# Attention and two feed-forward layers on one core: how the decay rows and the first q and k are brought in

## The chip, the cores and the metric

The kernel runs on one core of one Trainium2 chip. The metric is the device time of one execution in microseconds (us); the time before is the median of three runs. A core has five engines that work side by side, each through its own list of instructions in order: TensorE (PE in the profile, with its weight loads as PEld), VectorE (DVE), ScalarE (ACT), GpSimd (POOL) and SyncE (SP), which here issues transfers only.

## What is computed

Cut to what matters, with B, H, S, D = 4, 8, 576, 64, a model width of 512 and an inner width of 2048:

```python
scores = (q @ k.transpose(0, 1, 3, 2)) / sqrt(D)
log_f = log(clip(f, 1e-4, 1.0))              # f: [B, H, S]
cum = cumsum(log_f, axis=-1)
decay = cum[:, :, :, None] - cum[:, :, None, :]
scores = where(causal, -1e9, scores + decay)
attn = softmax(scores)                       # sum + 1e-9
x = (attn @ v)  as [B*S, H*D] = [2304, 512]
h = x @ w1_in;  g = h * tanh(softplus(h));  y = g @ w1_out
h = y @ w2_in;  g = h * cos(h);             out = g @ w2_out
```

q, k, v and f come as float32; the four weight matrices come as 64-bit floats, which the kernel takes apart into two float32 numbers each.

## The kernel before

**Jobs.** Attention goes by jobs: one pair of heads of one batch (`jobs`, L385 to L388). In batch 0 each pair is cut into two jobs, of query blocks 0 and 1 and of blocks 2, 3 and 4, so that the first four jobs need columns 0 to 255 only; in the other batches a pair is one job of 576 queries. That makes 20 jobs. `span` (L396) gives a job's batch, pair, first query and last key.

**The stacked operand.** The decay is added within the score product. For each job there is a tile `stk` of [128, 2 heads, 2, 576], two in a ring (`ring`, L635), in which index 0 of the third axis is for the queries and 1 for the keys. Rows 0 to 63 hold q (times 0.125) or k with the head's width along the rows; row 64 and row 96 hold the running sum `cum` or constants, so that the product adds cum of the query and takes off cum of the key. All other rows from 64 on are set by memsets once at the start (L639 to L642): 0, 0, -1 and 1. The product (`scores`, L501) runs over all 128 rows.

**Decay rows before.** `decay_tables` (L712) loads f as [32, 576], clips it (L716), takes the logarithm (L717) and the running sum over 576 columns (L719). `prep_job` begins with two transfers of one row each (L449, L450) for its own job: from the table in SBUF for job 0, for all others from `cumd`, a copy of the table in DRAM that job 0's preparation writes (L452).

**A job's preparation.** `load_job` (L401) brings q and k of a job as they lie; `prep_job` (L441) transposes them on TensorE (L468) into a PSUM bank and copies the result into `stk`, the queries of the first head on VectorE (L486), the other three parts on ScalarE (L484). At its end it starts the loads of v for the next job and of q and k for the job behind that. It is a generator, run a step at a time in the last steps of the job before. `load_v` (L420) brings v, which is needed by the product with the probabilities (`av`, L602).

**Softmax.** Per block: the score products, then on VectorE the mask, the negated values and the row minimum in one instruction (L529), on ScalarE the exponential with the row sum (L534), the reciprocal on VectorE, the scaling on GpSimd (L548), transposes on TensorE (L575, L591), copies of these into the tile `p` of probabilities (L567 on ScalarE, L569 on VectorE), and the product with v (L613).

**Weights.** `split_weights` (L88) brings weights in pieces into three buffers `raw` (L104); each piece takes three instructions on VectorE (L123, L124, L133), one on GpSimd (L128) or ScalarE, one on ScalarE (L137) and one on GpSimd (L138). The first pieces are converted between the softmax steps. Their loads are issued after the copy of the table to DRAM (`marks["cum"]`, L107).

**The order.** The main loop (L771 on) mixes attention steps, weight pieces and steps of the first feed-forward layer, by a credit per attention step. Within this a scheduler orders the instructions of every engine when the program is built; an engine then runs its list strictly in that order, and so does SyncE with the transfers that it issues. A transfer also waits until the one eight places ahead of it has landed.

Of the kernel before, what the change touches and what calls it, by code (L numbers as in the profile page):

```python
# [9 lines left out]
F32 = mybir.dt.float32  # L10
F32R = mybir.dt.float32r
I32 = mybir.dt.int32
AF = mybir.ActivationFunctionType
ALU = mybir.AluOpType
# [22 lines left out]
def tile_attention_two_ffn(  # L37
# [12 lines left out]
    nc = tc.nc  # L50
    B, H, S, D = q.shape
# [25 lines left out]
    xd = dram.tile([128, 2, NK, NT], F32, name="xd")  # L77
    yd = dram.tile([128, 2, NK, NT], F32, name="yd")
    pd = dram.tile([128, NK, NT], F32, name="pd")
    cumd = dram.tile([B * H, S], F32, name="cumd")  # L80


    W = {}
# [300 lines left out]
    def attention_units(p, bank):  # L384
# [16 lines left out]
        def load_job(jb):  # L401
            if jb >= len(jobs):
                return
            b, hp, qlo, khi, last = span(jb)
            hs = slice(2 * hp, 2 * hp + 2)
            ts = []
            for nm, src, lo in (("q", q, qlo), ("k", k, 0)):
                P, C = SPLIT[khi - lo]
                t = p.tile([128, 6, 2, D], F32, tag=f"nat{nm}", name=f"nat{nm}", bufs=2)
                if jb == 0:  # L410
                    nc.sync.dma_start(out=t[0:P, 0:C], in_=src[b, hs, lo:khi].rearrange("h (p c) d -> p c h d", c=C))
                else:
                    for j in range(2):
                        nc.sync.dma_start(
                            out=t[0:P, 0:C, j], in_=src[b, 2 * hp + j, lo:khi].rearrange("(c p) d -> p c d", c=C)
                        )
                ts.append(t)
            nat[jb] = ts

        def load_v(jb):  # L420
# [17 lines left out]
                        )  # L438
            vt[jb] = t

        def prep_job(jb):  # L441
            if jb >= len(jobs):
                return
            b, hp, qlo, khi, last = span(jb)
            qn, kn = nat.pop(jb)
            st = ring[jb % len(ring)]
            h0 = b * H + 2 * hp
            src = cums[0][h0 : h0 + 2] if jb == 0 else cumd[h0 : h0 + 2]
            nc.sync.dma_start(out=st[96:97, :, 0], in_=src)  # L449
            nc.sync.dma_start(out=st[64:65, :, 1], in_=src)  # L450
            if jb == 0:
                marks["cum"] = nc.sync.dma_start(out=cumd, in_=cums[0])  # L452
            yield
            cols = []
            for which, src, lo in ((0, qn, qlo), (1, kn, 0)):
# [9 lines left out]
            for g in groups:  # L465
# [3 lines left out]
                for which, lo in ((0, qlo), (1, 0)):  # L469
# [5 lines left out]
                    for j in range(2):  # L475
                        i_ = t[64 * j : 64 * j + 64, at : at + n * P]
                        if jb == 0:
                            o = st[0:64, j, which, lo:khi].rearrange("r (p c) -> r c p", c=C)[:, c0 : c0 + n]
                            i_ = i_.rearrange("r (c p) -> r c p", p=P)
                        else:  # L480
                            o = st[0:64, j, which, lo + c0 * P : lo + (c0 + n) * P]
                        sc = 0.125 if which == 0 else 1.0
                        if which or j:
                            nc.scalar.activation(out=o, in_=i_, func=AF.Copy, scale=sc)  # L484
                        else:
                            nc.vector.tensor_scalar(out=o, in0=i_, scalar1=sc, scalar2=None, op0=ALU.mult)  # L486
                yield
            if jb:
                load_v(jb + 1)
            load_job(jb + 2)  # L490

        def scores(jb, i):
# [6 lines left out]

            def product(o, j, c0, c1):  # L500
                marks["score"] = nc.tensor.matmul(  # L501
                    o, lhsT=st[:, j, 0, qs], rhs=st[:, j, 1, c0:c1], start=True, stop=True
                )

            heads = []
# [127 lines left out]
            nc.sync.dma_start(out=xd[:, :, hp, b * S + qlo : b * S + khi], in_=f(xs.pop(jb)[:, :, qlo:khi]))  # L633

        ring = []  # L635
        for i in range(2):
            ring.append(p.tile([128, 2, 2, S], F32, name=f"stk{i}", bufs=1))
            en = nc.vector if i == 0 else nc.gpsimd
            nc.gpsimd.memset(ring[-1][96:128, :, 0], 0.0)  # L639
            nc.gpsimd.memset(ring[-1][64:96, :, 1], 0.0)  # L640
            en.memset(ring[-1][64:96, :, 0], -1.0)
            en.memset(ring[-1][96:128, :, 1], 1.0)  # L642
            if i == 0:
                make_masks()
        for jb in range(2):
            load_job(jb)
        load_v(0)
        load_v(1)
        for _ in prep_job(0):
            pass  # L650
        prep = None
# [39 lines left out]
            nxt = [e for e in ends if e > m]  # L691
            yield ("step", m, nxt[0] - m if nxt else 1)

    nc.scalar.preload_act_table_set("natural_log_exp_and_others")
    make_identity(nc, ident)
    nc.gpsimd.memset(two, 2.0)
    nc.gpsimd.memset(quarter, 0.25)

    def make_masks():
        nc.gpsimd.memset(maskt, 0.0)  # L700
        nc.gpsimd.affine_select(
# [9 lines left out]

    def decay_tables(p):  # L712
        NH = B * H
        ft, cum, one = (p.tile([128, S], F32, tag="s", name="s", bufs=7)[0:NH] for _ in range(3))
        nc.sync.dma_start(out=ft, in_=fg.rearrange("b h s -> (b h) s"))
        nc.vector.tensor_scalar(out=ft, in0=ft, scalar1=1e-4, scalar2=1.0, op0=ALU.max, op1=ALU.min)  # L716
        nc.scalar.activation(out=ft, in_=ft, func=AF.Ln)  # L717
        nc.gpsimd.memset(one, 1.0)
        nc.vector.tensor_tensor_scan(out=cum, data0=one, data1=ft, initial=0.0, op0=ALU.mult, op1=ALU.add)  # L719
        cums.append(cum)  # L720

    NA = 8
    first = [(TA * i, TA, 2) for i in range(NA)]
# [38 lines left out]
    def bank():  # L762
        return psa.tile([128, 512], F32, tag="s1", name="s1")

    decay_tables(ap)
    att = attention_units(ap, bank)
    w1a = weights = split_weights(1, lo, w0p)
    done_tokens, attention_over, pos = 0, False, 0
    psf, credit = None, 0.0
# [75 lines left out]
```

## Time and profile before

| | |
|---|---|
| median of three runs | 1099.02 us (1098.57 to 1100.02) |
| the profiled execution's own time | 1097.69 us |
| its span, first to last instruction | 1095.9 us |
| mean granted TensorE clock | 0.998 |
| VectorE busy, share of the span | 637.9 us, 58% |
| ScalarE busy | 563.5 us, 51% |
| GpSimd busy | 232.8 us, 21% |
| packets of the transfers, share of 16 engines | 32.9% |

Times in the rows further down are in us from the start of the span. An instruction's line (L501) is its line in the kernel before. A float32 product shows as two records. "x4" are instructions of a kind that follow each other, merged into one row, with the time from the first one's start to the last one's end or their sum. The releaser named behind an idle time is inferred from the semaphores.

### The profile page before, as it was taken

Reading aid. Unit: us, or ns where it says so; the run is one execution under the profiler, and the core shown is the slowest. Engines: PE = TensorE matmul, PEld = TensorE weight load, DVE = VectorE, ACT = ScalarE, POOL = GpSimd, SP = SyncE. Lnnn points to the kernel's source line nnn. Section 1 sums busy time; section 2 is a strip of 40 time slices with the busy share of each in tenths; the row PEclk is TensorE's granted clock in tenths of the full one; section 3 lists DMA queues with packets and bytes.
Section 4 is the critical chain, followed back from the end, with each engine's and each line's share of the span. In section 5 each row is a group of like instructions: output and inputs, shape, how many; then the busy total and the mean of one; then the engine's idle time right before and its main releaser. Section 6 shows DMA issues by size and latency. Waiting matters only on the chain.

```text
span 1095.9 us, 17795 instructions
## 1 busy us (share of the span) xinstructions
PE 1062.1 (97%) x6496; PEld 936.1 (85%) x6496; DVE 637.9 (58%) x1461; ACT 563.5 (51%) x1196; POOL 232.8 (21%) x267
## 2 busy tenths in 40 slices
PE   5899999999999999999999999999999999999998
PEld 4575787688878889999999999889999999999987
DVE  5769675677547575543555525995444454454543
ACT  4676676766666564443444424665334343343432
POOL 6647532333322323221111101330000000000000
PEclk9999999999999999999999999999999999999999
DMA  5845522532251135454555535432010020100000
GB/s 138 218 116 151 173 56 75 156 85 55 75 151 35 56 131 182 166 193 130 159 188 185 180 121 188 155 105 87 1 58 30 1 87 1 58 29 1 31 1 29
DMA packets 119415, 110.54 MB, mean 101 GB/s; under 512 B 65168, under 2 KB 101520, under 8 KB 119328
## 3 DMA queue, kind: packets, MB, share of 16 engines
q1 hardware_dynamic: 119328, 109.41, 32.9%
q8 instruction: 51, 0.84, 0.3%
q14 instruction: 36, 0.29, 0.1%
HBM read 80.99 MB, written 28.39 MB: 100 GB/s over the span
## 4 chain that ended last, share of the span: by engine, by line
PE 85%; DVE 8%; issue 2%; ACT 2%; DMA 1%; SPq 1%; POOL 0%; ACTq 0%; POOLq 0%; DVEq 0%
PE h L205 20%; PE acc L227 17%; PE acc L236 17%; PE hx L205 14%; PE s L501 7%; PE s L613 5%; PE s L591 4%; PE s L468 1%; DVE raw L123 1%; DVE s L529 1%; DVE raw L124 1%; DVE raw L133 1%; ACT stk L484 1%; DMA xd<-xs 0%; DVE r L325 0%
## 5 line engine op out<-in xcount | busy, mean ns | idle before, releaser
L205 PE MATMUL h<-x,wih 128*128 128x384 f32 (+1 forms) x1056 | 242.1, 317 | 0.0
L343 DVE TENSOR_TENSOR gl<-e,gh 128x384 fp32r<-128x384 f32 (+1 forms) x157 | 108.6, 692 | 141.2 <-ACT gh L335 140.6
L205 PEld LDWEIGHTS h<-x,wih 128*128 128x128 f32 x1056 | 180.8, 189 | 8.7 <-issue 2.6
L205 PE MATMUL h<-x,wil 128*128 128x384 f32 (+1 forms) x528 | 167.5, 317 | 0.2 <-POOL wil L138 0.2
L205 PE MATMUL hx<-x,wih 128*128 128x384 f32 (+1 forms) x672 | 166.1, 328 | 0.0
L335 ACT ACTIVATE gh<-e 128x384 fp32r<-128x384 f32 (+1 forms) x180 | 97.8, 544 | 101.8 <-DVE e L331 53.8
L227 PE MATMUL acc<-gl,woh 128*128 128x256 f32 (+1 forms) x480 | 148.7, 310 | 0.0
L227 PE MATMUL acc<-gh,woh 128*128 128x256 f32 (+1 forms) x480 | 148.5, 312 | 0.0
L227 PE MATMUL acc<-gh,wol 128*128 128x256 f32 (+1 forms) x480 | 147.5, 308 | 0.0
L548 POOL TENSOR_SCALAR s<-s,sm 128x448 f32<-128x448 f32 (+5 forms) x144 | 92.1, 655 | 155.8 <-DVE sm L546 49.6
L501 PE MATMUL s<-stk 128*128 128x192 f32 (+7 forms) x384 | 111.9, 420 | 13.3 <-DMA stk<-s 4.5
L205 PEld LDWEIGHTS hx<-x,wih 128*128 128x128 f32 x672 | 120.1, 188 | 4.2
L236 PE MATMUL acc<-woh,gl 128*128 128x512 f32 x288 | 113.3, 397 | 3.1 <-DVE gl L343 3.1
L236 PE MATMUL acc<-wol,gh 128*128 128x512 f32 x288 | 113.7, 395 | 0.0
L236 PE MATMUL acc<-woh,gh 128*128 128x512 f32 x288 | 112.3, 390 | 0.8 <-DVE part L272 0.8
L205 PE MATMUL hx<-x,wil 128*128 128x384 f32 (+1 forms) x336 | 110.4, 328 | 0.0
L534 ACT ACTIVATE s<-s,mx 128x448 f32<-128x448 f32 (+5 forms) x144 | 83.5, 581 | 45.9 <-DVE mx L529 44.8
L205 PEld LDWEIGHTS h<-x,wil 128*128 128x128 f32 x528 | 99.8, 189 | 1.6 <-issue 0.6
L316 ACT ACTIVATE n<-n 128x384 f32<-128x384 f32 x96 | 50.4, 525 | 87.1 <-DVE n L305 87.1
L227 PEld LDWEIGHTS acc<-gl,woh 128*128 128x128 f32 x480 | 90.9, 189 | 2.6 <-issue 0.7
L227 PEld LDWEIGHTS acc<-gh,woh 128*128 128x128 f32 x480 | 90.7, 190 | 2.4 <-issue 1.1
L227 PEld LDWEIGHTS acc<-gh,wol 128*128 128x128 f32 x480 | 91.0, 190 | 1.8 <-issue 0.9
(88 smaller groups left out, 1669.1 us busy)
## 6 DMA issues: line engine op xcount, KB each, us to landing
raw<-in_moe_w_in_dram SPq DMA_DIRECT2D x32, 512.0 KB
raw<-in_moe_w_out_dram SPq DMA_DIRECT2D x32, 512.0 KB
x<-xd SPq DMA_DIRECT2D x6, 1536.0 KB
x<-yd SPq DMA_DIRECT2D x6, 1536.0 KB
x<-xd SPq DMA_DIRECT2D x8, 1024.0 KB
xd<-xs SPq DMA_DIRECT2D x12, 576.0 KB
natk<-in_k_dram SPq DMA_DIRECT2D x32, 144.0 KB
pd<-part SPq DMA_DIRECT2D x18, 256.0 KB
```

The source lines that it names most:

```text
L123: nc.vector.tensor_scalar(out=low, in0=low, scalar1=29, scalar2=None, op0=ALU.logical_shift_right)
L205: nc.tensor.matmul(o, lhsT=a[wsl], rhs=b[:, kk, :], start=(kk == 0 and i == 0), stop=(kk == NK - 1 and i == 2),)
L227: nc.tensor.matmul(o, lhsT=a[dsl], rhs=b[:, gs], start=(start and i == 0 and d % nsub == 0), stop=(end and i == 2), skip_group_check=True,)
L236: nc.tensor.matmul(acc[ti][m], lhsT=a[:, ms], rhs=b[:, j, :], start=(start and i == 0), stop=(end and i == 2),)
L316: nc.scalar.activation(out=t, in_=t, func=AF.Sin, scale=TWO_PI)
L335: nc.scalar.activation(out=gh, in_=e, func=AF.Copy)
L343: marks["v1"] = nc.vector.tensor_tensor(out=gl, in0=st[n][0], in1=f(gst[n][0]), op=ALU.subtract)
L501: marks["score"] = nc.tensor.matmul(o, lhsT=st[:, j, 0, qs], rhs=st[:, j, 1, c0:c1], start=True, stop=True)
L534: nc.scalar.activation(out=s[:, 0:w], in_=s[:, 0:w], func=AF.Exp, scale=-1.0, bias=mx, accum_out=sm[:, j : j + 1])
L548: nc.gpsimd.tensor_scalar(out=s[:, 0:w], in0=s[:, 0:w], scalar1=sm[:, j : j + 1], scalar2=1.0, op0=ALU.mult, op1=ALU.mult)
L591: nc.tensor.transpose(t[:, 128 * x : 128 * x + 128], ss[j][:, QS[c] : QS[c] + 128], ident)
L613: nc.tensor.matmul(t[64 * j : 64 * j + 64, c0:width], lhsT=vt[jb][0:kr, c, j], rhs=pt[0:kr, j, c, c0:width], start=(c == 0), stop=(c == nb ...
```

## The change

First, q and k of job 0 are issued by ScalarE, ahead of everything else that it does. Second, the rows move: `stk` now uses row 64 and row 65 only, the product runs over 66 rows, and there is one memset of -1 and one of 1 per ring tile. Jobs 0 and 1 get their rows from the table in SBUF, one row per transfer and only the columns that the job needs; from job 2 on there is one transfer per job from a DRAM table that holds both rows with their constants (`cumd`, now [2, 32, 2, 576], written by four transfers). A job's rows are asked for at the end of the preparation of the job before it, not at the start of its own. Third, clip, logarithm and running sum go by two parts, columns 0 to 255 and 256 to 575. Also, the copy of k for the first head of job 0 goes to VectorE, and masks, loads and memsets of the start stand in another order in the source.

```diff
-    cumd = dram.tile([B * H, S], F32, name="cumd")
+    cumd = dram.tile([2, B * H, 2, S], F32, name="cumd")
...
                 if jb == 0:
-                    nc.sync.dma_start(out=t[0:P, 0:C], in_=src[b, hs, lo:khi].rearrange("h (p c) d -> p c h d", c=C))
+                    nc.scalar.dma_start(out=t[0:P, 0:C], in_=src[b, hs, lo:khi].rearrange("h (p c) d -> p c h d", c=C))
...
+        def load_rows(jb):
+            if jb >= len(jobs):
+                return
+            b, hp, qlo, khi, last = span(jb)
+            st = ring[jb % len(ring)]
+            h0 = b * H + 2 * hp
+            if jb < 2:
+                for which in range(2):
+                    nc.sync.dma_start(out=st[64 + which : 65 + which, :, which, 0:khi], in_=cums[0][h0 : h0 + 2, 0:khi])
+            else:
+                nc.sync.dma_start(
+                    out=st[64:66].rearrange("x j w s -> x (j w s)"),
+                    in_=cumd[:, h0 : h0 + 2].rearrange("x j w s -> x (j w s)"),
+                )
+
+        def store_tables():
+            cum, one, less = cums
+            for x, which, src in ((0, 0, cum), (0, 1, one), (1, 0, less), (1, 1, cum)):
+                marks["cum"] = nc.sync.dma_start(out=cumd[x, :, which], in_=src)
...
-            h0 = b * H + 2 * hp
-            src = cums[0][h0 : h0 + 2] if jb == 0 else cumd[h0 : h0 + 2]
-            nc.sync.dma_start(out=st[96:97, :, 0], in_=src)
-            nc.sync.dma_start(out=st[64:65, :, 1], in_=src)
             if jb == 0:
-                marks["cum"] = nc.sync.dma_start(out=cumd, in_=cums[0])
+                load_rows(0)
             yield
...
-                        if which or j:
+                        if j if jb == 0 else which or j:
                             nc.scalar.activation(out=o, in_=i_, func=AF.Copy, scale=sc)
...
+            load_rows(jb + 1)
+            if jb == 0:
+                store_tables()
+                load_v(1)
             if jb:
                 load_v(jb + 1)
...
-                    o, lhsT=st[:, j, 0, qs], rhs=st[:, j, 1, c0:c1], start=True, stop=True
+                    o, lhsT=st[0:66, j, 0, qs], rhs=st[0:66, j, 1, c0:c1], start=True, stop=True
...
+        load_job(0)
+        yield ("begun", 0)
         for i in range(2):
...
-            nc.gpsimd.memset(ring[-1][96:128, :, 0], 0.0)
-            nc.gpsimd.memset(ring[-1][64:96, :, 1], 0.0)
             en.memset(ring[-1][64:96, :, 0], -1.0)
-            en.memset(ring[-1][96:128, :, 1], 1.0)
-            if i == 0:
-                make_masks()
-        for jb in range(2):
-            load_job(jb)
+            en.memset(ring[-1][64:96, :, 1], 1.0)
+        make_masks()
+        load_job(1)
         load_v(0)
-        load_v(1)
...
-        nc.vector.tensor_scalar(out=ft, in0=ft, scalar1=1e-4, scalar2=1.0, op0=ALU.max, op1=ALU.min)
-        nc.scalar.activation(out=ft, in_=ft, func=AF.Ln)
         nc.gpsimd.memset(one, 1.0)
-        nc.vector.tensor_tensor_scan(out=cum, data0=one, data1=ft, initial=0.0, op0=ALU.mult, op1=ALU.add)
-        cums.append(cum)
+        nc.gpsimd.memset(less, -1.0)
+        for c0, c1 in ((0, 256), (256, S)):
+            c = slice(c0, c1)
+            nc.vector.tensor_scalar(out=ft[:, c], in0=ft[:, c], scalar1=1e-4, scalar2=1.0, op0=ALU.max, op1=ALU.min)
+            nc.scalar.activation(out=ft[:, c], in_=ft[:, c], func=AF.Ln)
+            nc.vector.tensor_tensor_scan(
+                out=cum[:, c], data0=one[:, c], data1=ft[:, c], initial=cum[:, c0 - 1 : c0] if c0 else 0.0,
+                op0=ALU.mult, op1=ALU.add,
+            )
+        cums.extend((cum, one, less))
```

The built order at three places. First, SyncE's list from its start to the first weights, before; `s` is the tile of gates or of their sums, `stk_99` and `stk_115` are the two ring tiles, for jobs 0, 2, ... and 1, 3, ...:

```order
L715 DMA s<-in_f_dram 32x576
L411 DMA natq<-in_q_dram 64x8x64
L411 DMA natk<-in_k_dram 64x8x64
L414 DMA natq<-in_q_dram 64x4x64 x2
L414 DMA natk<-in_k_dram 64x4x64 x2
L436 DMA natv<-in_v_dram 128x2x64 x4
L449 DMA stk_99<-s 1x2x576
L450 DMA stk_99<-s 1x2x576
L452 DMA cumd<-s 32x576
L414 DMA natq<-in_q_dram 64x4x64 x2
L414 DMA natk<-in_k_dram 64x4x64 x2
L449 DMA stk_115<-cumd 1x2x576
```

The same place now (`stk_108` is the tile of jobs 0, 2, ..., `stk_111` that of jobs 1, 3, ...; L449 and L451 are the two transfers of `load_rows`):

```order
L727 DMA s<-in_f_dram 32x576
L414 DMA natq<-in_q_dram 64x4x64 x2
L414 DMA natk<-in_k_dram 64x4x64 x2
L436 DMA natv<-in_v_dram 128x2x64 x2
L449 DMA stk_108<-s 1x2x256 x2
L449 DMA stk_111<-s 1x2x256 x2
L459 DMA cumd<-s 32x576 x4
L436 DMA natv<-in_v_dram 128x2x64 x2
L414 DMA natq<-in_q_dram 64x4x64 x2
L414 DMA natk<-in_k_dram 64x4x64 x2
L104 DMA raw<-in_moe_w_in_dram 128x2x512 x2
L104 DMA raw<-in_moe_w_out_dram 128x1024
```

The two loads of job 0 have left SyncE; two of the four loads of v stand behind the rows, and the rows of both first jobs ahead of the table stores. Right behind these rows the list goes on so, with the row transfer of job 2 directly behind the weights, and that of job 3 behind the loads of job 3:

```order
L451 DMA stk_108<-cumd 2x2304
L414 DMA natq<-in_q_dram 64x4x64 x2
L414 DMA natk<-in_k_dram 64x4x64 x2
L451 DMA stk_111<-cumd 2x2304
L414 DMA natq<-in_q_dram 80x4x64 x2
```

In the list before, the two row transfers of job 2 stood behind the loads of job 3 (L414), which stood behind the weights.

Second, VectorE at the first piece of weights (`raw`), before; the copies L486 go into `stk`, here that of job 2, and L529 is the mask and minimum, here of job 1's two blocks:

```order
L529 ISA s,mx<-s_229,maskt 128x128
L529 ISA mx 128x1
L123 TENSOR_SCALAR raw<-raw 128x512
L486 TENSOR_SCALAR stk_99<-s_246 64x256
L124 SCALAR_TENSOR_TENSOR raw<-raw 128x512
L545 TENSOR_SCALAR sm<-sm 128x2
L123 TENSOR_SCALAR raw<-raw 128x512
```

The same place now (L549 is the mask and minimum, L589 the copy of transposed probabilities, L502 the copy into `stk`):

```order
L549 ISA s,mx<-s_271,maskt 128x256
L549 ISA mx 128x1
L123 TENSOR_SCALAR raw<-raw 128x512
L589 COPY p<-s_293 128x2x128
L502 TENSOR_SCALAR stk_108<-s_249 64x256
L124 SCALAR_TENSOR_TENSOR raw<-raw 128x512
L565 TENSOR_SCALAR sm<-sm 128x2
```

Job 1's second block (`s_271`, 256 columns) is now reduced ahead of the first weight operation, and a copy of probabilities stands between that and job 2's copy.

Third, TensorE at the same time, before; L468 are the transposes of q and k, L501 the score products, L591 the transposes of probabilities:

```order
L501 MATMUL s_229<-stk_115 128x128 x2
L468 MATMUL s_246<-ident,natq 128x64 x4
L468 MATMUL s_246<-ident,natk 128x64 x4
L501 MATMUL s_268<-stk_115 128x256 x2
L591 MATMUL s_289<-ident,s 128x128 x2
L501 MATMUL s_298<-stk_99 128x128 x2
```

And now (L484, L521 and L611 in their place):

```order
L521 MATMUL s_234<-stk_111 128x128 x2
L484 MATMUL s_249<-ident,natq 128x64 x4
L521 MATMUL s_271<-stk_111 128x256 x2
L611 MATMUL s_293<-ident,s 128x128 x2
L484 MATMUL s_249<-ident,natk 128x64 x4
L521 MATMUL s_302<-stk_108 128x128 x2
```

The transposes of k for job 2 have moved behind job 1's second block; job 2's first products come last in both. Further on the lists differ in small exchanges of neighbours only, and from some 280 us of the trace before on, TensorE's list is the same.

## Rows read from the trace of the kernel before

**Rows 1.** The page, totals: busy time (share of the span) and instructions by engine.

```profile
PE 1062.1 (97%) x6496; PEld 936.1 (85%) x6496; DVE 637.9 (58%) x1461; ACT 563.5 (51%) x1196; POOL 232.8 (21%) x267
```

**Rows 2.** Table by stages: length, PE, PEld, DVE, ACT, POOL busy, PEclk, DMA share, GB/s.

```profile
30.00:60.00 30.00, 25.94 (x172) 18.62 (x171) 21.99 (x74) 21.39 (x57) 18.95 (x23) 0.94 0.78 202
...
130.00:200.00 70.00, 69.38 (x493) 53.33 (x493) 43.99 (x151) 47.07 (x121) 22.16 (x33) 1.00 0.35 90
```

**Rows 3.** Timeline, 0 to 13 us: start, length, instruction, [idle before, releaser].

```profile
0.72 1.28 ACT L694 ACT_TABLE_LOAD   x1 [0.72 <-PEq L830]
0.73 0.40 SPq L715 DMA_DIRECT2D s<-in_f_dram  x1
1.19 0.73 SPq L411 DMA_DIRECT2D natq<-in_q_dram  x1
1.96 0.64 SPq L411 DMA_DIRECT2D natk<-in_k_dram  x1
...
3.00 1.05 POOL L640 MEMSET stk<- 32x1152 f32 x1
3.38 0.98 DVE L716 TENSOR_SCALAR s<-s 32x576 f32<-32x576 f32 x1
...
4.39 0.68 ACT L717 ACTIVATE s<-s 32x576 f32<-32x576 f32 x1 [2.38 <-DVE s L716]
...
5.16 0.69 PE L468 MATMUL s<-ident,natk 64*128 64x64 f32 x4 [0.30 <-DMA natk<-in_k_dram]
5.18 1.35 DVE L719 TENSOR_TENSOR_SCAN s<-s 32x576 f32<-32x576 f32 x1 [0.82 <-POOL mask L705]
...
5.31 2.14 SPq L436 DMA_DIRECT2D natv<-in_v_dram  x4
...
7.06 1.89 ACT L484 ACTIVATE stk<-s 64x256 f32<-64x256 f32 x3 [1.99 <-DVE stk L486]
...
8.44 0.62 SPq L450 DMA_DIRECT2D stk<-s  x1
...
9.81 0.53 POOL L707 TENSOR_SCALAR_AFFINE_SELECT mask<-mask 64x64 f32<-64x64 f32 x2
...
10.30 1.19 PE L501 MATMUL s<-stk 128*128 128x128 f32 x4 [4.46 <-DMA stk<-s]
```

**Rows 4.** Timeline, 13 to 25 us: the first weights, and job 2's copies and first products.

```profile
13.77 0.91 SPq L104 DMA_DIRECT2D raw<-in_moe_w_in_dram  x2
...
17.74 0.43 DVE L123 TENSOR_SCALAR raw<-raw 128x512 int32<-128x512 int32 x1 [0.83 <-DMA raw<-in_moe_w_in_dram]
...
18.08 0.41 DVE L486 TENSOR_SCALAR stk<-s 64x256 f32<-64x256 f32 x1
...
18.58 1.19 ACT L484 ACTIVATE stk<-s 64x256 f32<-64x256 f32 x3 [0.96 <-DVE stk L486]
...
23.06 1.20 PE L501 MATMUL s<-stk 128*128 128x128 f32 x4 [3.28 <-DMA stk<-cumd]
```

**Rows 5.** Chain of waits, 0 to 90 us: start, length, what the end waited for.

```profile
18.73 4.20 DMA stk<-cumd
...
70.50 4.59 DMA xd<-xs
```

**Rows 6.** TensorE: two timeline rows, then the stage table (length, busy, PEclk, DMA share, GB/s).

```profile
12.46 2.07 PE L501 MATMUL s<-stk 128*128 128x256 f32 x4
...
31.76 1.05 PE L501 MATMUL s<-stk 128*128 128x256 f32 x4
...
30.80:47.90 17.10, 13.42 (x86) 1.00 0.86 218
...
48.00:51.00 3.00, 2.72 (x6) 0.50 0.43 98
```

**Rows 7.** TensorE's weight loads by form, 130 to 383 us: busy us, mean ns | idle before.

```profile
L591 PEld LDWEIGHTS s<-ident,s 128*128 128x128 f32 x298 | 32.6, 140 | 10.0 <-issue 6.8 <-POOL s L548 1.2
L468 PEld LDWEIGHTS s<-ident,natk 96*128 96x128 f32 x60 | 6.5, 140 | 0.1
```

More of the change, by code (lines that the diff above doesn't have):

```diff
@@ L692, in attention_units @@
             yield ("step", m, nxt[0] - m if nxt else 1)
[L694 to L697, printed above, removed]
     def make_masks():
@@ L713, in decay_tables @@
         NH = B * H
-        ft, cum, one = (p.tile([128, S], F32, tag="s", name="s", bufs=7)[0:NH] for _ in range(3))
+        ft, cum, one, less = (p.tile([128, S], F32, tag="s", name="s", bufs=7)[0:NH] for _ in range(4))
         nc.sync.dma_start(out=ft, in_=fg.rearrange("b h s -> (b h) s"))
-        nc.vector.tensor_scalar(out=ft, in0=ft, scalar1=1e-4, scalar2=1.0, op0=ALU.max, op1=ALU.min)
-        nc.scalar.activation(out=ft, in_=ft, func=AF.Ln)
         nc.gpsimd.memset(one, 1.0)
-        nc.vector.tensor_tensor_scan(out=cum, data0=one, data1=ft, initial=0.0, op0=ALU.mult, op1=ALU.add)
-        cums.append(cum)
+        nc.gpsimd.memset(less, -1.0)
[8 more added lines that the diff above has]
+        cums.extend((cum, one, less))
     NA = 8
@@ L763, in bank @@
         return psa.tile([128, 512], F32, tag="s1", name="s1")
+    att = attention_units(ap, bank)
+    next(att)
+    nc.scalar.preload_act_table_set("natural_log_exp_and_others")
+    make_identity(nc, ident)
+    nc.gpsimd.memset(two, 2.0)
+    nc.gpsimd.memset(quarter, 0.25)
     decay_tables(ap)
-    att = attention_units(ap, bank)
     w1a = weights = split_weights(1, lo, w0p)
```

## The prediction

> **What bounds the kernel now.** The engine totals come first: TensorE is busy for 1062.1 us of a span of 1095.9 us [rows 1], so a change that touches no matrix product of the two feed-forward layers can move little beyond the 33.8 us in which it is idle. The table by stages says where those lie: from 130 to 200 us 0.62 of 70 us are idle, from 30 to 60 us alone 4.06 of 30 [rows 2]. So the end is set by how soon TensorE is fed without gaps, and all that follows is about the first 130 us.
>
> The timeline of the start comes next; a row's bracket says how long the engine was idle before it and what ended that. TensorE stands idle for 4.46 us until the first job's decay rows have landed. The path to them: VectorE's clip of the gates at 3.38 us, logarithm 0.68, running sum 1.35 us, over at 6.53. But SyncE issues four loads of v first (5.31 to 7.45), the second of the two row transfers goes out at 8.44, and the first product starts at 10.30, 1.86 us after it [rows 3]. The timeline from 13 us on has the other large gap, 3.28 us: the third job's copies are over at 19.77 us (18.58 + 1.19), yet its product waits until 23.06 for rows of the table [rows 4]; in the chain of waits that transfer is one piece of 4.20 us from 18.73 on [rows 5].
>
> **The change, part by part.**
>
> *First q and k on ScalarE.* q is issued at 1.19 us on SyncE, behind the gates, and k 0.77 later [rows 3]. On ScalarE I expect 0.73, as the gates have it, and 1.50, so both land 0.46 us sooner: k, whose transposes start at 5.16, at 4.7. No row shows an issue on ScalarE; SyncE's go from 0.40 to 0.73 us [rows 3], and I take the 0.73, of the same transfer. Two of them stand before the activation table load of 1.28 us, which then ends near 3.5; the logarithm has its input at 3.85, and that covers it. A rule speaks against this part: the Trainium skill, DMA: Bandwidth & Descriptors, section Issuing engines are not separate DMA queues, has it that issuing from a second engine saves only the time of issuing. By it q and k gain the same 0.46 us; if the row were to show a shorter flight as well, the sum would not change, because the rows land last either way.
>
> *Decay sums in two parts.* Taken by columns from [rows 3]: clip 0.45 and 0.55, logarithm 0.35 and 0.43, sum 0.60 and 0.75 us. The first clip runs from 3.38 to 3.85, the first logarithm to 4.25, the second clip to 4.45, the first sum from 4.50 to 5.15, where the whole sum ended at 6.53. The starts of the three extra instructions lie within the rounding; the second sum falls between two copies.
>
> *First rows from SBUF, 256 columns.* SyncE issues the gates, four loads for job 1 (0.65 each) and two loads of v, and is free at 4.95 instead of 7.45 us. Rows go out at 5.2 and 5.95 and land at 5.95 + 1.86 = 7.8 us. The first job's copies alternate in the built program, each waiting for the one before: VectorE 5.4 to 5.95, ScalarE (0.63, a third of 1.89) to 6.6, the second sum on VectorE to 6.75, its second copy to 7.3, ScalarE's second to 7.95. So the first product starts near 8.1 us, 2.2 us sooner. GpSimd loses four memsets of 1.05 us ahead of the masks and gains one of half that size; the masks, over at 10.34 us before (9.81 + 0.53), are ready near 6.7, which the first product covers.
>
> *One row transfer per job, a job earlier.* Two issues become one in 18 jobs, and three table stores are added (0.40, as the gates' issue). On SyncE the first weights now stand behind four row transfers, four stores, two loads of v and four of q and k: 7.95 + 1.7 + 1.0 + 2.6 gives 13.3 us, against 13.77 [rows 4]. The transfer for job 2 follows the three weight loads, at 14.7 us; what it waits for, the second block's products of job 0, ended at 14.53 before [rows 6] and should end at 12.3. No row shows a transfer of two pieces of 9 KB. The nearest are 1.73 us on quiet queues (the 1.86 less 0.13 until the product starts [rows 3]) and 4.20 and 4.59 us under load [rows 5]: it lands between 16.4 and 19.3 us. I take 19, since it flies among weights. Behind it on SyncE stand the loads of job 3, not needed before 20 us.
>
> What is late next for job 2 is its copies. VectorE takes its instructions in order: the first weight operation, which waited 0.83 us for its load until 17.74 [rows 4], then a copy out of the bank of probabilities, and only then the copy for job 2. With the load 0.5 us sooner and job 1's reductions now ahead of it, the weight operation runs from 17.4 to 17.8, the other copy to 18.3, the copy for job 2 (0.41) to 18.8, ScalarE's three (1.19) to 20.0, and the product starts at 20.2 instead of 23.06: 2.9 us sooner. The gain of the start is inside this, not beside it.
>
> *66 rows in the score products, not 128.* TensorE's weight loads of 96 rows take 140 ns, those of 128 rows 140 [rows 7]: nothing.
>
> *Sum.* The profiled execution took 1097.69 us (span 1095.9 and 1.79 around it); less 2.9 that is 1094.8. The median of the three runs, 1099.02, stands 1.33 above that execution, so for the median the forecast is **1096.1 us**. About 0.2% (2.2 us) is what a measurement of this kernel can tell from no change.
>
> **Rivals.**
>
> *More is gained (1093.5 us).* If the weights land sooner than reckoned, VectorE doesn't hold job 2's copies back, and both gaps go one beside the other: 2.2 + 3.3 = 5.5 us. For it: rows are no longer last. Against: VectorE's order, weights first.
>
> *The gain is eaten before 130 us (1098.5 us).* The first weights come only 0.5 us sooner, and VectorE, busy 21.99 of the 30 us from 30 to 60 [rows 2], converts them between the softmax steps. If conversion, not the products, sets the pace until the feed-forward starts, 0.5 us is all that is left. For it: VectorE's share there, which the change doesn't lower. Against: its softmax part starts sooner and leaves conversion room.
>
> *The clock rises later (1106 us, slower).* Four passes of the same product take 2.07 us at 12.46 and 1.05 us at 31.76 [rows 6]: TensorE ran at the lower of its two levels, 1.2 GHz, first and at 2.4 GHz then. From 48 to 51 us the granted clock is 0.50 again [rows 6]. If job 2's products come sooner but with new gaps behind them, the rise may come later. From 30.8 to 47.9 us TensorE works 13.42 and is idle 3.68 us [rows 6]; all of that work at the lower level adds 13.42 less the idle time, 9.7 us, against 2.9 gained: 6.8 us slower. It decides if the rise comes some 5 us later than now (2.9 over 9.7/17.1 for each). For it: the new order puts transposes of k between score products. Against: less waiting before 30 us, not more. The Trainium skill, TensorE: Matmul & The Clock Gate, Part 1, says that the array starts at half rate and goes back to it after idling. The trace agrees, with 0.50 from 48 us on; by this rule the time could come out either way.
>
> *The change doesn't do what it says* would mean rows that still land last for job 2. With one transfer at 14.7 us in place of two around 18 I leave that inside the second rival.
>
> **How the numbers follow.** Forecast near 2.9 us: 0.47. More: 0.15. Eaten: 0.26. Slower: 0.12. So faster by over 0.2%: 0.62, within 0.2%: 0.26, slower by over 0.2%: 0.12. The range goes from 1092.0 us (5.5 us and 1.5 for the bounds of issue and landing) to 1100.0 (all eaten and one new gap of 1 us); the slower case lies outside. The forecast's own range is 1094.5 to 1097.5.
>
> **What would show it.** Right: the first score product at 8.0 to 8.3 us; job 2's at 19.5 to 20.5 behind its copies; no wait of over 0.5 us for rows of the table; the first weight operation on VectorE near 17.4; the products' times halving some 3 us sooner; the feed-forward's first product 2 to 3 us sooner; the stages behind 130 us as they are. Wrong: a row transfer that still ends a long wait of TensorE, a feed-forward that starts at the same time as before, or a longer time at 0.50.

## The result, and the profile after

The changed kernel took **1111.18 us** (median of 4 runs, 1110.86 to 1112.04); the kernel before, run beside it, took 1099.07 (1098.57 to 1100.02). The ratio is 1.0117, with a 95% interval of 1.0104 to 1.0129: some 12 us slower, where 3 us faster was forecast. The profiled execution took 1111.44 us, with a span of 1109.7 us.

The totals of the page after, against [rows 1], say what kind of loss it is:

```profile
PE 1081.1 (97%) x6496; PEld 947.6 (85%) x6496; DVE 642.3 (58%) x1464; ACT 563.0 (51%) x1196; POOL 225.5 (20%) x264
```

TensorE runs the same 6496 instructions and is busy 19.0 us longer (1081.1 less 1062.1). Its idle time is 28.6 us (1109.7 less 1081.1) where it was 33.8, so 5.2 us of waiting did go. 19.0 less 5.2 is the whole 13.8 us by which the span grew. The changed kernel waits less and works longer at the same work: that points at the speed of TensorE.

Where this happens is seen in the timeline of TensorE. First two rows of the kernel before, then the same two of the kernel after: the score products over 448 columns, and the first products of the feed-forward (L205).

```profile
37.03 2.55 PE L501 MATMUL s<-stk 128*128 128x448 f32 x6
...
51.25 0.74 PE L205 MATMUL h<-x,wih 128*128 128x256 f32 x2
```

```profile
39.25 4.75 PE L521 MATMUL s<-stk 66*128 66x448 f32 x6
...
58.89 1.31 PE L205 MATMUL h<-x,wih 128*128 128x256 f32 x2
```

Six products of the same columns take 4.75 us in place of 2.55. At 39 us the changed kernel still works at 1.2 GHz, where the kernel before had gone over to 2.4 [rows 6], and it still does so at 58.89 us: the pair of products there, which the change does not touch, takes 1.31 us and not 0.74. The feed-forward starts 7.64 us later.

The table by stages (columns as in [rows 2]) has the rest, first after, then one stretch of before:

```profile
30.00:60.00 30.00, 28.82 (x98) 16.95 (x97) 16.67 (x60) 16.93 (x45) 14.06 (x19) 1.00 0.58 145
...
107.00:120.50 13.50, 12.55 (x61) 8.30 (x62) 12.30 (x31) 7.39 (x20) 9.15 (x9) 0.50 0.43 110
```

```profile
107.00:120.50 13.50, 13.49 (x102) 10.46 (x103) 12.92 (x32) 10.08 (x27) 13.01 (x13) 1.00 0.50 156
```

From 30 to 60 us TensorE is busy for 28.82 us, more than the 25.94 of [rows 2], and gets through 98 instructions instead of 172. (The 1.00 for the clock there is no evidence: the trace has no record of the clock before its first rise, and the column then prints 1.00. The durations tell the level, as in [rows 6].) From 107 to 120.5 us the granted clock is 0.50, the lower of its two levels, and 61 instructions run where 102 did. By the chain of waits a run of 48 products of L205 starts at 220.39 us before and at 231.92 after, 11.5 us later:

```profile
220.39 5.76 PE h L205 x48
```

```profile
231.92 5.77 PE h L205 x48
```

So 7.6 us of the 13.8 are lost up to the feed-forward and 3.9 more by 220 us; the remaining 2.3 us further on were not followed up.

The start went much as forecast. The timeline of the first 9 us after, by the steps of the prediction:

```profile
1.46 0.67 ACTq L411 DMA_DIRECT2D natk<-in_k_dram  x1
...
4.72 0.67 DVE L734 TENSOR_TENSOR_SCAN s<-s 32x256 f32<-32x256 f32 x1
...
5.41 2.74 SPq L449 DMA_DIRECT2D stk<-s  x4
...
5.72 0.69 PE L484 MATMUL s<-ident,natk 64*128 64x64 f32 x4 [1.17 <-DMA natk<-in_k_dram]
...
8.38 1.45 PE L521 MATMUL s<-stk 66*128 66x128 f32 x4 [1.98 <-DVE stk L502]
```

The first score product starts at 8.38 us (10.30 in [rows 3]), and it waits for a copy, no longer for the rows. k was issued 0.50 us sooner and its transposes started 0.56 us later than in [rows 3], and the copies wait for them. Then job 2, to be read against [rows 4]:

```profile
13.93 0.60 SPq L104 DMA_DIRECT2D raw<-in_moe_w_in_dram  x1
...
15.65 0.26 SPq L451 DMA_DIRECT2D stk<-cumd  x1
...
18.07 0.43 DVE L123 TENSOR_SCALAR raw<-raw 128x512 int32<-128x512 int32 x1 [0.21 <-DMA raw<-in_moe_w_in_dram]
...
18.75 0.41 DVE L502 TENSOR_SCALAR stk<-s 64x256 f32<-64x256 f32 x1
19.25 1.18 ACT L500 ACTIVATE stk<-s 64x256 f32<-64x256 f32 x3 [0.61 <-DVE stk L502]
...
21.75 1.19 PE L521 MATMUL s<-stk 66*128 66x128 f32 x4 [3.66 <-DMA stk<-cumd]
```

The copies for job 2 are over at 20.43 us (19.25 + 1.18), but the product waits until 21.75 for its rows, 6.1 us after their issue at 15.65.

### The profile page after: what moved, and what is told of

Same layout as the page of the kernel before. It is cut to its first block, busy times and chain, and to the rows that moved or that the text cites. A ratio compares the mean times of both kernels' runs of the same rounds, so it can differ in the third digit from the quotient of the medians.

```text
span 1109.7 us, 17774 instructions
## 1 busy us (share of the span) xinstructions
PE 1081.1 (97%) x6496; PEld 947.6 (85%) x6496; DVE 642.3 (58%) x1464; ACT 563.0 (51%) x1196; POOL 225.5 (20%) x264
## 4 chain that ended last, share of the span: by engine, by line
PE 87%; DVE 6%; DMA 2%; ACT 2%; issue 2%; POOL 1%; SPq 0%; ACTq 0%; DVEq 0%; POOLq 0%
PE h L205 20%; PE acc L227 17%; PE acc L236 17%; PE hx L205 14%; PE s L521 8%; PE s L633 6%; PE s L611 4%; PE s L484 1%; DMA raw<-in_moe_w_out_dram 1%; DVE raw L133 1%; ACT stk L500 1%; DVE raw L124 1%; DVE raw L123 1%; DVE s L549 1%; POOL wil L138 1%
## 5 line engine op out<-in xcount | busy, mean ns | idle before, releaser
L205 PE MATMUL h<-x,wih 128*128 128x384 f32 (+1 forms) x1056 | 245.8, 320 | 0.0
L205 PEld LDWEIGHTS h<-x,wih 128*128 128x128 f32 x1056 | 182.8, 191 | 10.1 <-issue 3.6
L205 PE MATMUL h<-x,wil 128*128 128x384 f32 (+1 forms) x528 | 168.2, 319 | 0.0
L205 PE MATMUL hx<-x,wih 128*128 128x384 f32 (+1 forms) x672 | 166.2, 328 | 0.0
L521 PE MATMUL s<-stk 66*128 66x192 f32 (+7 forms) x384 | 120.1, 446 | 10.3 <-DMA stk<-cumd 3.7
L205 PEld LDWEIGHTS hx<-x,wih 128*128 128x128 f32 x672 | 120.1, 188 | 4.2
L568 POOL TENSOR_SCALAR s<-s,sm 128x448 f32<-128x448 f32 (+5 forms) x144 | 89.3, 634 | 165.6 <-DVE sm L566 55.3
L205 PE MATMUL hx<-x,wil 128*128 128x384 f32 (+1 forms) x336 | 110.4, 328 | 0.0
L205 PEld LDWEIGHTS h<-x,wil 128*128 128x128 f32 x528 | 100.9, 191 | 1.4 <-POOL wil L138 0.2
```

The source lines that it names most:

```text
L205: nc.tensor.matmul(o, lhsT=a[wsl], rhs=b[:, kk, :], start=(kk == 0 and i == 0), stop=(kk == NK - 1 and i == 2),)
L521: marks["score"] = nc.tensor.matmul(o, lhsT=st[0:66, j, 0, qs], rhs=st[0:66, j, 1, c0:c1], start=True, stop=True)
L568: nc.gpsimd.tensor_scalar(out=s[:, 0:w], in0=s[:, 0:w], scalar1=sm[:, j : j + 1], scalar2=1.0, op0=ALU.mult, op1=ALU.mult)
```

## The experiments

**Theories.** The change has two parts that could have to do with the clock. Theory A: the products that drive 66 rows instead of 128 hold the clock down. Theory B (the rival of the prediction): the new order and its gaps do. The first two kernels tell them apart, each with one of the two parts alone.

**The change with 128 rows.**

```diff
-                    nc.sync.dma_start(out=st[64 + which : 65 + which, :, which, 0:khi], in_=cums[0][h0 : h0 + 2, 0:khi])
+                    nc.sync.dma_start(out=st[96 - 32 * which : 97 - 32 * which, :, which, 0:khi], in_=cums[0][h0 : h0 + 2, 0:khi])
...
-                    o, lhsT=st[0:66, j, 0, qs], rhs=st[0:66, j, 1, c0:c1], start=True, stop=True
+                    o, lhsT=st[0:128, j, 0, qs], rhs=st[0:128, j, 1, c0:c1], start=True, stop=True
...
-            en.memset(ring[-1][64:96, :, 1], 1.0)
+            en.memset(ring[-1][96:128, :, 1], 1.0)
```

(With it go the transfers from the table into rows 64 and 96, and the two memsets of zeros of the kernel before.)

> The change with score products over 128 rows again: decay rows at 64 and 96, zeros and ones around them by memsets as before, still one row transfer per job, ScalarE's loads and the sums in two parts. Theory A (the clock rises late because the score products drive 66 rows of the array and not 128): the products' times halve before 33 us and 1095 to 1099 us in all. Theory B (it rises late because of the new order and its gaps, whatever the rows): low level until about 60 us as in the change, 1108 to 1113 us.

Measured: 1097.41 us (1095.95 to 1100.34, 10 runs), ratio to before 0.9998 (0.9985 to 1.0011). The whole loss is gone, with everything else of the change in place. Timeline of TensorE and one stretch of the stage table:

```profile
8.14 1.40 PE L521 MATMUL s<-stk 128*128 128x128 f32 x4 [2.02 <-DVE stk L502]
...
21.89 1.20 PE L521 MATMUL s<-stk 128*128 128x128 f32 x4 [3.75 <-DMA stk<-cumd]
...
37.95 2.55 PE L521 MATMUL s<-stk 128*128 128x448 f32 x6
...
50.85 0.75 PE L205 MATMUL h<-x,wih 128*128 128x256 f32 x2
```

```profile
107.00:120.50 13.50, 13.48 (x103) 10.49 (x100) 12.91 (x31) 9.97 (x26) 13.01 (x13) 1.00 0.50 154
```

The order is that of the change, the gap ahead of job 2's product is the same 3.7 us, and yet the six products take 2.55 us and the clock from 107 us on is 1.00. Theory B falls. (Short falls to the lower level are no sign of the loss: the kernel before has one from 48 to 51 us [rows 6], this one from 31.5 to 34.7 us.) The rows also show what the rest of the change is worth: a lead of 2.16 us at the first product, of 1.17 at job 2's, of 0.40 at the feed-forward, and nothing at the end.

**The kernel before with 66 rows.**

```diff
-            nc.sync.dma_start(out=st[96:97, :, 0], in_=src)
-            nc.sync.dma_start(out=st[64:65, :, 1], in_=src)
+            nc.sync.dma_start(out=st[64:65, :, 0], in_=src)
+            nc.sync.dma_start(out=st[65:66, :, 1], in_=src)
...
-                    o, lhsT=st[:, j, 0, qs], rhs=st[:, j, 1, c0:c1], start=True, stop=True
+                    o, lhsT=st[0:66, j, 0, qs], rhs=st[0:66, j, 1, c0:c1], start=True, stop=True
```

(As in the change, the two memsets of zeros go, and that of 1 moves to row 64.)

> The kernel before with only its score products changed: decay rows at 64 and 65, products over 66 rows; loads, transfers and sums as before. Theory A: a late rise of the clock here too, 1106 to 1113 us. Theory B: the rise stays near 31 us, 1098 to 1100 us.

Measured: 1110.71 us (1105.26 to 1112.19, 4 runs), ratio 1.0103 (1.0070 to 1.0137): the loss of the change, from this one edit. Its timeline, with the product that [rows 6] show at 31.76 us, and its stage table:

```profile
31.83 1.97 PE L501 MATMUL s<-stk 66*128 66x256 f32 x4
...
38.85 4.75 PE L501 MATMUL s<-stk 66*128 66x448 f32 x6
...
56.54 1.31 PE L205 MATMUL h<-x,wih 128*128 128x256 f32 x2
```

```profile
107.00:118.00 11.00, 10.65 (x51) 6.74 (x52) 10.51 (x26) 4.39 (x14) 8.51 (x8) 0.50 0.46 140
```

Four passes of the same product start within 0.07 us of where they did, and take 1.97 us instead of 1.05. So theory A holds, in both directions.

**96 and 97 rows.** Does every row count, or whole quarters of the array? 97 rows reach into the last quarter, 96 don't. The kernel with 96 is the change with `st[0:96]` and no other edit, that with 97 is the one with 128 rows but

```diff
-                    o, lhsT=st[0:128, j, 0, qs], rhs=st[0:128, j, 1, c0:c1], start=True, stop=True
+                    o, lhsT=st[0:97, j, 0, qs], rhs=st[0:97, j, 1, c0:c1], start=True, stop=True
```

> The change with products over rows 0 to 95: rows 66 to 95 hold -1 and 1 and add the same constant to all scores of a row, which the softmax takes out; no other instruction differs, and the built order is that of the change until about 250 us. Theory A, if rows count one by one: a rise between that of 66 rows and of 128, 1098 to 1109 us. Theory C (the fourth group of 32 rows counts, and 66 rows already use three): as the change, 1110 to 1112 us. Theory B: as the change.

> As e1 but with products over rows 0 to 96 only, so that one row of the fourth group of 32 is in use. Theory A, rows one by one: as e3 within 2 us. Theory C: as e1, 1095 to 1099 us. Theory B: as the change, 1108 to 1113 us.

Measured: 1105.05 us with 96 rows (ratio 1.0052, 1.0033 to 1.0072) and 1103.51 with 97 (1.0048, 1.0032 to 1.0064). The two are alike, and both lie between 66 rows and 128. Timelines of TensorE, 66 rows (the change), then 96, then 97, and for comparison 128 rows and the kernel before:

```profile
36.30 0.63 PE L611 MATMUL s<-ident,s 128*128 128x128 f32 x2
```

```profile
36.29 0.42 PE L611 MATMUL s<-ident,s 128*128 128x128 f32 x2
...
38.24 2.55 PE L521 MATMUL s<-stk 96*128 96x448 f32 x6
...
103.38 2.17 PE L633 MATMUL s<-p,natv 64*64 64x256 f32 x8
```

```profile
37.38 2.55 PE L521 MATMUL s<-stk 97*128 97x448 f32 x6
...
110.18 0.63 PE L205 MATMUL h<-x,wih 128*128 128x256 f32 x2
```

```profile
103.59 1.23 PE L633 MATMUL s<-p,natv 64*64 64x256 f32 x8
```

```profile
110.34 0.40 PE L205 MATMUL h<-x,wih 128*128 128x256 f32 x2
```

At 36.3 us the change and its twin with 96 rows start the same pair of transposes within 0.01 us of each other, and only the twin is on its way to the higher level. Both kernels in between, with 96 and 97 rows, have that level by 38 us and lose it again near 100 us: the eight products of L633 take 2.17 us for 1.23 with 128 rows, the pair of L205 0.63 us for 0.40 before. From 100 to 130 us the mean granted clock is 0.77 with 66 rows, 0.83 with 96, 0.80 with 97 and 1.00 with 128. The last quarter does not decide. The loss goes roughly with the rows left out, 1.17% for 62 of them and 0.52 and 0.48% for 32 and 31; four points show no finer law.

**128 rows, filled with zeros.** Is it that rows are driven, or what they hold?

```diff
-            en.memset(ring[-1][64:96, :, 0], -1.0)
-            en.memset(ring[-1][96:128, :, 1], 1.0)
+            en.memset(ring[-1][64:96, :, 0], 0.0)
+            en.memset(ring[-1][96:128, :, 1], 0.0)
+            en.memset(ring[-1][64:65, :, 0], -1.0)
+            en.memset(ring[-1][96:97, :, 1], 1.0)
```

> As e1, but the rows that only fill up the product hold 0 in both operands (before, one operand held 0 and the other 1 or -1). Two more memsets on VectorE at the start cost 2 us for job 0. Theory A1 (rows driven, whatever they hold): the products' times halve before 36 us as in e1, 1096 to 1101 us. Theory A2 (what the rows hold counts): the low level lasts beyond 45 us, 1104 to 1113 us.

Measured: 1099.4 us (one run, 1098.47 before). Its first product starts 2.7 us later than with constants (8.14), and the first pair of the feed-forward, later too, is at the higher level:

```profile
10.87 1.19 PE L521 MATMUL s<-stk 128*128 128x128 f32 x4 [4.55 <-DMA stk<-s]
...
54.53 0.75 PE L205 MATMUL h<-x,wih 128*128 128x256 f32 x2
```

No 12 us are lost, so rows of zeros do nearly what rows of constants do. Whether they do quite as much, one run that also starts later can't tell.

**Where the gain of the start goes.** Three kernels start from the one with 128 rows. The first brings the first weights ahead of the table stores; the second fills the gaps of TensorE with twelve products of the identity, whose result nobody reads; the third does both, with ten of them.

```diff
+                load_job(2)
+                marks["cum"] = marks["rows"]
+                next(w1a)
...
```

```diff
...
+        filler(3)
         for _ in prep_job(0):
             pass
+        filler(3)
...
+                    if items[m2] == (2, 0):
+                        with tc.issue_after(marks["turn"].ins):
+                            filler(6)
```

(The first also brings the loads of job 2 forward, and lets `split_weights` stop after its first three loads; `filler(n)` issues n products of the identity into a bank of its own.)

> As e1, but the loads of q and k of job 2 and the first three weight loads are issued right behind the rows of jobs 0 and 1, ahead of the table stores and the loads of v. Theory D (in e1 the gain of the start is eaten because the first weights land no sooner, and their conversion paces the chain from 19 us to the feed-forward): the first weight operation on VectorE 2 to 3 us sooner than the 19.1 us of e1, the feed-forward's first product 1.5 to 3 us sooner than 50.9, and 1 to 3 us less in all than the kernel before. Theory E (it is eaten by the rows of job 2 or by the clock): the feed-forward within 1 us of e1 and no difference to the kernel before.

> As e1, with twelve products of the identity with itself (128 by 128, into a bank that nobody reads) where TensorE is idle: three ahead of the first transposes, three between those of q and of k, six between job 2's transposes and its first products. They add nothing to the result. If the clock follows how gapless TensorE's work is, it rises before 28 us for good; if the clock alone ate the gain, 1 to 3 us less than the kernel before; if the weights pace the chain (D), the feed-forward's first product stays within 1 us of e1 and the time with it.

> e6 and e7 together (ten filling products). If clock and weights each hold part of the gain: 2 to 5 us less than the kernel before, and more than either alone; if one of them is the whole cause, as that one alone.

Measured: weights early 1099.24 us, ratio 1.0004 (0.9994 to 1.0014); filled 1097.70, 0.9993 (0.9984 to 1.0002); both 1099.19, 1.0004 (0.9991 to 1.0016). None differs from before. Timeline with early weights, SyncE and TensorE:

```profile
20.67 1.11 SPq L456 DMA_DIRECT2D stk<-cumd  x2
...
23.09 0.76 PE L529 MATMUL s<-stk 128*128 128x128 f32 x2 [6.69 <-ACT wih L142]
```

Weights moved forward push job 2's row transfer back, from 15.79 us to 20.67, and the product starts at 23.09, as late as in [rows 4]. The first weight operation did come sooner, at 15.95 us instead of 19.09, but the feed-forward starts at 52.22, later than with 128 rows alone, so this run does not tell its two theories apart. (The releaser named, a weight operation, is not an input of this product; the row transfer is.) With filled gaps the clock is up before job 2 comes, and the feed-forward starts 1.05 us sooner than in the kernel with 128 rows alone:

```profile
21.77 0.68 PE L526 MATMUL s<-stk 128*128 128x128 f32 x4 [1.55 <-DMA stk<-cumd]
...
49.80 0.76 PE L205 MATMUL h<-x,wih 128*128 128x256 f32 x2
```

Even this, 1.45 us ahead of the kernel before, does not show in the time: its interval holds 1.

**First q and k by SyncE again.** The kernel with 128 rows and

```diff
-                    nc.scalar.dma_start(out=t[0:P, 0:C], in_=src[b, hs, lo:khi].rearrange("h (p c) d -> p c h d", c=C))
+                    nc.sync.dma_start(out=t[0:P, 0:C], in_=src[b, hs, lo:khi].rearrange("h (p c) d -> p c h d", c=C))
```

> The change with 128 rows (e1), but with the first q and k issued by SyncE again, behind the gates. If ScalarE's issue is what brings the first product forward, k lands later by about the 0.5 us of issue and SyncE reaches the decay rows and the weights two issues later (some 1.4 us): first product 8.6 to 9.5 us against 8.14 in e1, first weight operation after 20.0 us. If k's flight and not its issue sets the start of the transposes (in the changed kernel k was issued sooner and did not land sooner), the first product stays within 0.4 us of 8.14. The time: within 0.2% of e1 (1097.4 us) by both, since the start's gain is gone by 50 us in e1.

Measured: 1100.84 us (1097.80 to 1102.78), ratio 1.0022 (1.0012 to 1.0033), against 0.9998 with ScalarE: outside both expectations. Timeline of the start, all engines:

```profile
0.73 0.75 SPq L411 DMA_DIRECT2D natq<-in_q_dram  x1
...
2.21 0.63 SPq L729 DMA_DIRECT2D s<-in_f_dram  x1
...
4.80 0.69 PE L484 MATMUL s<-ident,natk 64*128 64x64 f32 x4 [0.47 <-DMA natk<-in_k_dram]
...
9.61 1.63 DVE L736 TENSOR_TENSOR_SCAN s<-s 32x256 f32<-32x256 f32 x2 [0.69 <-POOL s L730]
...
13.12 1.19 PE L521 MATMUL s<-stk 128*128 128x128 f32 x4 [7.63 <-DMA stk<-s]
```

The edit did more than it says. The scheduler put the gates behind q and k, and GpSimd's memset for the sum behind those of the ring tiles and the masks, so the sum starts at 9.61 us and the first product at 13.12. This run does not price ScalarE's issue by itself. It does show that with 5 us lost at the first product the feed-forward starts 3.3 us later (54.18 us) and the end comes 3.4 us later (1100.84 against 1097.41, from two sessions; 2.6 us by the ratios to before), so the start is not without weight. It also shows k issued by SyncE at 1.54 us and used at 4.80, where ScalarE's issue at 1.46 was used at 5.43 with 128 rows.

**Job 2's row by GpSimd.** Again the kernel with 128 rows:

```diff
-                nc.sync.dma_start(
+                (nc.gpsimd if jb == 2 else nc.sync).dma_start(
                     out=st[64:97:32].rearrange("x j w s -> x (j w s)"),
```

> e1 with the one row transfer of job 2 issued by GpSimd instead of SyncE, where it stood behind three weight loads (issued 15.8, landed 21.6 us). Theory: the row is late because it flies behind the weights; issued ahead of or beside them it lands with under 3 us of flight and job 2's product waits for its copies only, at 20.0 to 20.8 us against 21.89. Rival: any transfer in this stretch takes 5 to 6 us, whoever issues it; then the product starts at 21 us or later. The time: by the prediction's sum 1.0 to 1.9 us less than e1; if all that is gained ahead of the feed-forward is eaten by the conversion of the weights, as e1 and e7 indicate, 1097.4 within 1 us.

Measured: 1099.76 us (1097.79 to 1101.00), ratio 1.0009 (0.9999 to 1.0018): above both times that were expected. Timeline from 13 us on:

```profile
13.26 0.73 POOL L451 DMA_DIRECT2D stk<-cumd  x1 [0.42 <-PE s L521]
...
18.84 0.41 DVE L502 TENSOR_SCALAR stk<-s 64x256 f32<-64x256 f32 x1
...
19.34 1.18 ACT L500 ACTIVATE stk<-s 64x256 f32<-64x256 f32 x3 [0.48 <-DVE stk L502]
...
20.16 0.80 PE L521 MATMUL s<-stk 128*128 128x128 f32 x2 [1.86 <-ACT stk L500]
...
25.19 0.66 PE L484 MATMUL s<-ident,natq 64*128 64x64 f32 x4 [2.95 <-DMA natq<-in_q_dram]
```

The transfer lands 2.6 us after its issue, and job 2's product starts at 20.16 us behind copies, as the prediction had it (20.2), though not behind all of them: ScalarE's last ends at 20.52. But the wait turns up one step later: 2.95 us for job 3's q, whose loads stand behind the weights, and the feed-forward starts at 52.55 us, later than before. The weights come later as well: the second piece's first operation on VectorE waits 2.34 us for its load and starts at 22.26 us, where it ran at 20.76 with 128 rows alone. The transfer was both issued by another engine and 0.8 us ahead of the weights (14.08 us); which of the two shortened its flight is not separated.

**Row by GpSimd and filled gaps.**

> e10's row on GpSimd together with e7's twelve extra products of the identity ahead of the first transposes and of job 2's products (these add nothing to the outputs). If the two gains add (e7: clock up at 18.8 us, feed-forward 1.05 us sooner than e1; e10: job 2's product 1 to 1.9 us sooner), 1095.5 to 1096.7 us, faster than before by 0.15 to 0.25%. If the conversion of the weights sets when the feed-forward starts, 1097.0 to 1098.0, the same as before.

Measured: 1097.49 us (1096.32 to 1099.92), ratio 0.9995 (0.9987 to 1.0004). Timeline of TensorE:

```profile
20.41 0.49 PE L526 MATMUL s<-stk 128*128 128x128 f32 x2
...
22.26 0.43 PE L489 MATMUL s<-ident,natq 64*128 64x64 f32 x4 [0.71 <-DMA natq<-in_q_dram]
```

Of both long waits 0.71 us is left, and still the feed-forward starts at 50.49 us and the time is that of before. So no version tried beats the kernel before by more than the measurement can tell.

## Why the prediction was wrong, by its steps

**The step that failed is the shortest one: 66 rows in place of 128, "nothing".** It priced the edit by the duration of a weight load [rows 7], and that reading was true. Weight loads of the score products by form, first before, then after, from 130 us on:

```profile
L501 PEld LDWEIGHTS s<-stk 128*128 128x128 f32 x216 | 35.0, 190 | 7.4 <-DVE p L569 1.7 <-issue 1.0 <-ACT p L567 0.8
```

```profile
L521 PEld LDWEIGHTS s<-stk 66*128 66x128 f32 x225 | 36.2, 190 | 9.2 <-DVE p L589 2.2 <-DVE xs L649 1.4 <-issue 1.1
```

190 ns each. The products take the same time too, once both are at the higher level: 539 ns over 448 columns from 130 to 383 us, with 128 rows as with 66. What it left out is that the rows bear on the level of the clock: the edit alone costs 12.75 us in the kernel before (1110.71 less 1097.96), and undoing it in the change gives 13.8 back (1111.18 less 1097.41, of two sessions). With this falls the frame of the whole prediction, that little can move beyond the 33.8 us in which TensorE is idle: its busy time itself grew by 19.0 us.

The Trainium skill, TensorE: Matmul & The Clock Gate, section LDWEIGHTS (loading the stationary operand), says that the time of a load goes by columns and not by rows; the 190 ns agree. Its Part 1 explains the clock by how busy the array has lately been, with idle time as what brings it down. Here the trace does not bear that out as the whole story: from 30 to 60 us TensorE was busy for 28.82 of 30 us after, more than before, and the products at 58.89 us still ran at 1.2 GHz.

**The rival "the clock rises later" had the outcome and not the cause.** It gave 1106 us: all work up to the end of the first fast stretch at the lower level. That part came true (7.64 us at the feed-forward); a second slow stretch from 107 to 120.5 us was not in it. But it made the rise hang on new gaps behind job 2, and the run with the same order and 128 rows has no such loss. Its argument against itself, "less waiting before 30 us, not more", was right, and the clock rose later all the same.

**First product, 8.1 us: right, in part by luck,** 8.38 and 8.14 with 128 rows. k was to land 0.46 us sooner and its transposes started 0.56 us later than before, 1.0 us behind the forecast. This carries through to the product, which follows them by 2.7 us in both kernels (5.72 and 8.38, 5.43 and 8.14). Against it stands that the product waits for three copies and not for all four: VectorE's second is over at 8.33 us, ScalarE's second only at 8.98.

**First weights, issue 13.3 us, operation 17.4: late by 0.6 and 0.7** (13.93 and 18.07; 14.06 and 19.09 with 128 rows).

**Job 2's product at 20.2 us: wrong by 1.55 us,** by the flight of the row transfer. It was bounded by 1.73 and 4.59 us, and took up to 6.1 behind the weights. It also went out at 15.65 us and not at 14.7, but with 4.59 us of flight it would still have landed by 20.3, ahead of the last copy. With a flight of 2.6 us the product started at 20.16, close to the 20.2 by two errors that cancel: the copies ended some 0.5 us later than reckoned (20.43, and 20.52 in that run), and the product did not wait for the last of them.

**2.9 us gained at the end: wrong also without the rows.** The prediction carried a lead at job 2 unchanged to the end. The rival "eaten before 130 us" (1098.5 us) is what the kernel with 128 rows shows: leads of 2.16, 1.17 and 0.40 us, then 0.9998. Its reason, the conversion of the weights, is borne out in part. The chain of waits of that kernel has, where the one before has the row transfer [rows 5], the first weight load and then its conversion:

```profile
14.06 5.00 DMA raw<-in_moe_w_in_dram
...
19.09 0.43 DVE raw L123
```

Of the 10 us from there to 29.04 us, 5.6 are weight operations of VectorE and GpSimd, and the first of them starts 1.35 us later than the 17.74 of [rows 4]. But this is one chain of one execution, and with the weights 3 us sooner nothing was gained, because job 2's row came late. What is shown is that each shortened wait is followed by another, for job 3's q in the run with GpSimd, and that 1.45 us of lead at the feed-forward (filled gaps) is no longer seen at the end. What takes that last lead stays open.

## What to carry to other kernels

An operand's unused rows cost TensorE no time, but leaving them out can cost clock: after such an edit compare the durations of untouched products at several places, not that of the edited one alone, and not at one place, since short falls of the clock occur in kernels without the loss, too. When busy time grows at an equal count of instructions, ask for the clock before asking for waits. A change of several parts is taken apart fastest in both directions: the change without one part, and the kernel before with that part alone.

## What the runs showed of the hardware that was not expected

- The rows that products drive bear on TensorE's clock, at unchanged durations at the higher level (190 ns a weight load, 539 ns a product of 448 columns): 1111.18 us with 66 rows, 1105.05 with 96, 1103.51 with 97, 1097.41 with 128. Rows of zeros do nearly as much (1099.4, one run). How the chip arrives at this is not shown.
- With 66 rows the lower level came back under load: TensorE was busy for 5.64 of the 7 us before, and for 12.55 of the 13.5 us from 107 us on at a granted clock of 0.50.
- A transfer of 18 KB behind three weight loads was waited for until 6.1 us after its issue; by another engine and ahead of them it took 2.6 us.
- Loads that two engines issue at once were no faster: k issued 0.50 us sooner was used 0.56 us later (0.27 us later with 128 rows).
